# A gated linear attention with a two-layer network on one core: another order of all engines, and v of the later units loaded through ScalarE's queue

## The chip, the cores and the metric

The kernel runs on 1 core of one Trainium2 chip. The metric is the device time of one execution in microseconds, the median over several runs. The core has five engines that run their own instruction lists in order and meet through semaphores: TensorE (PE, with its weight loads PEld), VectorE (DVE), ScalarE (ACT), GpSimd (POOL) and SyncE (SP), which here only issues transfers. Transfers run on 16 DMA engines.

## The reference

```python
# q, k, v, f_logit: [4, 8, 768, 48] float32
f = 1.0 / (1.0 + np.exp(-f_logit))
state = zeros((B, H, D, D)); y = zeros_like(q)
for t in range(S):
    state = f[:, :, t, :, None] * state + np.einsum('bhd,bhe->bhde', k[:, :, t], v[:, :, t])
    y[:, :, t] = np.einsum('bhd,bhde->bhe', q[:, :, t], state)
# x: the heads side by side, [3072, 384]; w_in [384, 2048]; w_out [2048, 384]
x = y.transpose(0, 2, 1, 3).reshape(B * S, H * D)
h = x @ w_in
out = np.maximum(0.01 * h, h) @ w_out
```

The forget gate f is different for every time step, head and channel, so the state is a decayed sum of outer products of k and v.

## The kernel before

The recurrence is computed in chunks of 128 time steps. A chunk needs the cumulative sum of log f (a matmul with a triangular matrix), k and q scaled by the exponentials of it, the scores k q under a causal mask, their product with v, and the product of q with the state before the chunk. The state at a chunk's end is carried to the next chunk of the same batch. Every 256 rows of the attention's result go through the two layers of the network, with a leaky relu between them.

The work is cut into 12 units of 256 rows. Units 0 to 3 are the first two chunks of one batch each (a "paired" unit, in which a partition holds two neighbouring time steps); units 4 to 11 are one chunk of two batches each. In step names the first number is the unit and the second the half (2 is both).

- `Lf`, `Lk`, `Lq`, `Lv` load f_logit, k, q, v of a unit (196,608 bytes a half) into one of six raw buffers; `WI_i`, `WO_i` load the quarters of the weights into the last two of these buffers, and `CI`, `CO` cast them to bf16.
- `ge`, `gl` (ScalarE, L211, L223) make log f; `cs` (PE, L232 to L243) sums it; `dec` (ScalarE, L251 to L257) makes the exponentials; `k`, `q` (VectorE or GpSimd, L263) scale; `v` (GpSimd, L268 to L277) casts v.
- `tk`, `tq`, `ck`, `cq` transpose k and q of units 0 to 3 through PE and copy them out (L296, L309, L311); for units 4 to 11 `xk`, `xq` (SP, L316) transpose by DMA.
- `sc` (PE, L332, L339) makes the scores, `mk` (VectorE, L349, L353) masks them, `mx` and `ms` (PE, L370) multiply by v and by the state, `xt` copies the result out.
- `pt` (PE, L435, L440) makes k v, `sf` (VectorE) and `sb` (GpSimd) update the state.
- `up` (PE, L468: 6 matmuls of 256 columns) is an eighth of the first layer of a unit, `pr` (ScalarE, L473) its relu, `dn` (PE, L480: 4 matmuls of 384 columns) a quarter of the second layer for 128 rows, `ob` copies the result out, `st` (SP, L515) stores it. `dh`, `oh`, `sh` do the last 128 rows in two column halves.
- `F_n` (PE, L133) are n matmuls on a constant whose result nobody reads. `zk`, `zv`, `zs`, `c0`, `pm`, `ut` set constants, among them the pair mask (`pm`).

Nothing plans at run time: the text `order` lists all steps, and each step is written out when its word is read. So the order of words is the order on each engine and in SP's queue. A number after `@` is the PSUM bank; a last number 0, 1 or 2 of `ck`, `cq`, `xt`, `ob`, `CI`, `CO` picks VectorE, ScalarE or GpSimd, and of `k`, `q`, `pm`, `zv`, `zs` 0 is VectorE and 1 GpSimd. Between engines the framework sets semaphores where a step reads or overwrites what another wrote. Each transfer also waits for the landing of the one that stands eight places before it, since eight semaphores are shared in turn.

```python
for word in order.split():
    word, _, at = word.partition("@")
    name, *numbers = word.split("_")
    parts[name](*[int(n) for n in numbers], *[int(n) for n in at.split(".") if n])
```

Of the kernel before, what the change touches and what calls it, by code (L numbers as in the profile page):

```python
# [15 lines left out]
def kernel(  # L16
# [134 lines left out]
    def raw(j, x):  # L151
        return (raw_fk if x in "fk" else raw_qv)[j % NB][:, "fkqv".index(x) % 2]

    def by_pair(t):
        return t.rearrange("t a h d -> t (a h d)").rearrange("t (h s d) -> t h s d", s=2, d=D)

    def load(x):
        def go(j, a):
            if paired(j):
                h = slice(0, H) if a == 2 else slice(4 * a, 4 * a + 4)  # L160
                nc.sync.dma_start(out=by_pair(raw(j, x))[:, h].rearrange("t h s d -> t h (s d)"),  # L161
                                  in_=srcs[x][j, h, 0:2 * C, :].rearrange("h (t s) d -> t h (s d)", s=2))
            else:
                c, h = units[j]
                nc.sync.dma_start(out=raw(j, x)[:, a],
                                  in_=srcs[x][2 * h + a, :, c * C:(c + 1) * C, :].rearrange("h t d -> t h d"))
        return go
# [393 lines left out]
    xt_4_1_1 up_5_5@3 Lf_8_1 Lf_9_0 sb_5_0 q_6_2_0 sf_4_1 Lq_8_1 xt_4_0_0 pr_5_5 pr_5_4 Lv_7_1 Lk_7_0 sb_4_1 up_5_6@4
    cs_7_1@7 k_6_2_0 Lk_7_1 sf_4_0 ob_2_0_0 dec_7_1 up_5_7@3 up_5_2@0 pr_5_6 sb_4_0 k_7_2_1 q_7_2_0 up_5_0@6 up_5_1@7
    pr_5_3 up_4_2@4 pr_5_0 up_4_6@2 up_4_1@1 up_4_4@5 pt_5_1@6 pr_5_1 up_4_0@7 xk_6 sf_5_1 pr_4_1 Lv_7_0 Lv_6_1 xq_6
    pr_5_7 up_4_7@1 pr_4_2 xk_7 v_7_2 pr_5_2 sb_5_1 xq_7 pr_4_0 ge_8_2 up_4_3@3 up_4_5@4 Lf_10_1 dn_5_0_0@6 pr_4_4
    dn_5_0_1 Lf_10_0 st_2_0 st_3_0 gl_8_2 pr_4_3 cs_8_0@0 pr_4_5 pr_4_7 pt_7_0@7 dn_4_0_0@5 dn_4_0_1 sf_7_0 pr_4_6
    dn_5_0_2 ge_9_2 dn_5_0_3 sc_6_1@3.4 dec_8_0 sc_6_0@1.7 sc_7_0@2.0 dn_4_0_2 mk_6_0_0 dn_4_0_3 Lf_11_1 mk_6_0_1
    mk_6_1_0 mk_7_0_0 ob_4_0_1 mk_6_1_1 ob_5_0_1 ge_10_2 dn_4_1_0@1 pt_7_1@7 cs_8_1@3 Lf_11_0 st_2_1 Lq_8_0 Lk_8_0
    gl_9_2 dn_4_1_1 v_6_2 dn_4_1_2 sc_7_1@5.2 gl_10_2 mx_6_0@6 Lq_9_0 mk_7_0_1 Lq_9_1 mk_7_1_0 mk_7_1_1 mx_6_1@4
    mx_7_0@0 xt_6_1_1 mx_7_1@5 xt_6_0_1 Lk_9_1 xt_7_0_0 cs_9_1@2 dn_4_1_3 sf_7_1 dn_5_1_0@4 ge_11_2 Lk_8_1 Lk_9_0
    st_3_1 Lv_9_1 up_6_5@6 pt_6_0@0 dec_8_1 ob_4_1_0 pr_6_5 xt_7_1_1 up_6_1@7 up_6_4@1 gl_11_2 sf_6_0 up_7_0@3  # L570
    cs_9_0@6 Lv_9_0 up_7_2@0 up_7_1@5 dec_9_1 Lv_10_1 up_7_5@2 q_8_2_0 dec_9_0 pr_7_0 pr_7_1 pt_6_1@6 up_7_4@3
    up_6_0@5 pr_6_4 up_7_3@1 pr_6_0 sb_7_0 Lk_11_1 q_9_2_1 sb_6_0 pr_7_2 sf_6_1 xq_8 Lv_10_0 Lv_8_1 k_8_2_0 up_6_2@6
    up_6_7@5 pr_7_4 up_7_6@0 pr_7_3 cs_10_1@3 dn_5_1_1 pr_6_1 dn_5_1_2 cs_11_0@1 pr_6_7 pr_7_6 dn_7_1_0@7 up_6_3@5
    up_7_7@0 dn_5_1_3 sb_7_1 k_9_2_1 xk_8 st_4_1 dec_11_0 pr_6_2 pr_7_5 dec_10_1 Lv_8_0 v_8_2 ob_5_1_0 dn_7_1_1
    Lq_11_1 Lk_11_0 sc_8_1@1.6 Lq_10_0 xk_9 sc_8_0@2.3 mk_8_1_0 dn_7_1_2 pt_8_1@4 sb_6_1 mk_8_0_0 xq_9 dn_6_0_0@1
    Lk_10_1 Lq_10_1 st_4_0 pr_7_7 pr_6_3 dn_6_0_1 pt_8_0@0 dn_6_1_0@5 mk_8_0_1 st_5_1 up_6_6@2 dn_6_1_1 Lk_10_0
    pr_6_6 sf_8_1 mk_8_1_1 v_9_2 sf_8_0 dn_6_1_2 dn_6_0_2 cs_10_0@3 Lq_11_0 Lv_11_1 sc_9_0@4.6 sc_9_1@0.2 dn_7_1_3
    mk_9_0_1 mk_9_1_0 cs_11_1@6 st_5_0 Lv_11_0 dn_6_1_3 mk_9_0_0 ob_7_1_0 dec_10_0 pt_9_0@3 mk_9_1_1 dn_6_0_3 sb_8_0
    mx_8_1@0 dec_11_1 q_11_2_1 k_10_2_1 mx_9_1@4 mx_9_0@6 xt_9_1_1 sf_9_0 ob_6_0_0 xq_11 mx_8_0@7 xt_8_0_0 q_10_2_0
    xt_9_0_1 dn_7_0_0@2 st_6_0 pt_9_1@3 xt_8_1_0 up_9_0@4 sf_9_1 dn_7_0_1 up_9_1@1 up_8_4@6 pr_9_0 xq_10 up_9_5@7  # L580
# [47 lines left out]
```

## Time and profile before

| | |
|---|---|
| median of 3 runs | 183.21 us (181.9, 183.21, 185.36) |
| profiled execution, its own time | 180.78 us |
| its span, first to last instruction | 179.0 us |
| busy: PE, ACT, DVE, POOL | 167.6, 108.1, 82.5, 72.3 us |
| granted TensorE clock | 1.000 over the span |
| read from HBM, written | 25.17 MB, 4.72 MB |
| instructions | 5543 |

The profile is one execution, taken by the hardware's profiler; all durations are read from it. Its own time is 1.78 us longer than its span, which is what lies before the first and after the last instruction. The runs beside it were timed without the profiler. A row of a timeline gives the start and length in us, engine, line, operation, what it writes and reads, and how many alike follow each other; in brackets stands how long the engine was idle before it and what ended that. "SPq" is SP's queue, where a row is the time that the issue of a transfer took, not the transfer. In the rows by line, three numbers with strokes are the shortest, median and longest duration in ns.

### The profile page before, as it was taken

What the parts mean: (1) busy time and instruction counts of PE and PEld (TensorE: products, weight loads), DVE (VectorE), ACT (ScalarE), POOL (GpSimd) and SP (SyncE); (2) the same over time, 40 slices, a digit from 0 to 9 for tenths busy, and PEclk for the clock granted to TensorE, in tenths of its full rate; (3) what the DMA queues carried; (4) which work ended last, traced back from release to release, by engine and by line L of the source; (5) the groups of instructions that cost most, each with busy time, mean ns of one, the idle gap of its engine ahead of it and who ended that gap; (6) DMA issues with size and microseconds to landing.
All of it is one profiled execution on the core that took longest, in us unless ns stands there. A gap on an engine that the chain in (4) does not pass through costs nothing.

```text
span 179.0 us, 5543 instructions
## 1 busy us (share of the span) xinstructions
PE 167.6 (94%) x2302; PEld 131.0 (73%) x2302; DVE 82.5 (46%) x172; ACT 108.1 (60%) x234; POOL 72.3 (40%) x143
## 2 busy tenths in 40 slices
PE   5698989999999999999799999977999999999993
PEld 1456779997567875899656898654798897786772
DVE  7299997644615305684047731363933910110001
ACT  3979766887266992586946878703338354451330
POOL 5177884566303950544570048082499100000000
PEclk9999999999999999999999999999999999999999
DMA  5999999998998999989899989999979000110204
GB/s 149 302 319 346 299 355 291 270 405 275 189 221 188 205 231 190 236 167 218 153 190 267 201 193 211 231 155 249 210 169 245 2 4 0 48 44 0 88 4 176
DMA packets 105961, 34.44 MB, mean 192 GB/s; under 512 B 100688, under 2 KB 103888, under 8 KB 105936
## 3 DMA queue, kind: packets, MB, share of 16 engines
q1 hardware_dynamic: 105936, 34.09, 79.4%
q8 instruction: 18, 0.29, 0.7%
q14 instruction: 7, 0.06, 0.1%
HBM read 25.17 MB, written 4.72 MB: 167 GB/s over the span
## 4 chain that ended last, share of the span: by engine, by line
PE 70%; DMA 12%; SPq 8%; issue 3%; DVE 3%; POOL 2%; ACT 0%; POOLq 0%; DVEq 0%
PE ps L468 31%; PE ps L480 27%; DMA raw_qv<-in_v_dram 7%; SPq L161 5%; PE ps L370 5%; DMA qT<-qh 5%; PE ps L339 2%; SPq L316 2%; POOL vb L268 1%; PE ps L240 1%; PE ps L440 1%; PE ps L296 1%; DVE wm L349 1%; PE ps L435 1%; DVE qh L263 1%
## 5 line engine op out<-in xcount | busy, mean ns | idle before, releaser
L473 ACT ACTIVATE gT<-ps 128x512 bf16<-128x512 f32 x96 | 52.7, 614 | 31.1 <-PE ps L468 28.9
L468 PE MATMUL ps<-xT,w_in 128*128 128x256 bf16 x576 | 69.7, 273 | 0.1
L480 PE MATMUL ps<-w_out,gT 128*128 128x384 bf16 x368 | 67.0, 326 | 0.0
L468 PEld LDWEIGHTS <-w_in 128*128 128x128 bf16 x576 | 61.7, 114 | 3.1 <-POOL w_in L184 0.2
L480 PEld LDWEIGHTS <-gT 128*128 128x128 bf16 x368 | 34.8, 98 | 19.4
L353 DVE TENSOR_TENSOR wm<-ps,ut 128x512 bf16<-128x512 f32 x32 | 20.1, 684 | 15.8 <-PE ps L339 15.6
L491 DVE COPY osb<-ps 128x384 f32<-128x384 f32 x13 | 7.2, 557 | 29.6 <-PE ps L480 28.7
L460 POOL CAST sb<-sf 64x192 bf16<-64x192 f32 x40 | 17.0, 425 | 4.5 <-DVE sf L450 2.4
L263 POOL TENSOR_TENSOR qh<-raw_qv,at 128x384 bf16<-128x384 f32 (+1 forms) x7 | 9.6, 1364 | 22.7 <-DMA raw_fk<-in_k_dram 11.8
L268 POOL CAST vb<-raw_qv 128x384 bf16<-128x384 f32 (+1 forms) x16 | 10.6, 663 | 16.1 <-DMA raw_qv<-in_v_dram 16.0
L452 DVE TENSOR_TENSOR sf<-sf,ps 64x192 f32<-64x192 f32 x32 | 11.2, 349 | 12.3 <-PE ps L440 10.6
L251 ACT ACTIVATE em<-ps 128x384 bf16<-128x384 f32 x24 | 12.0, 500 | 7.5 <-PE ps L240 3.9
L457 POOL TENSOR_TENSOR sf<-sf,end 128x192 f32<-128x192 f32 x16 | 8.8, 550 | 15.8 <-DVE sf L452 13.7
L422 ACT CAST xT<-ps 128x384 bf16<-128x384 f32 x16 | 7.9, 517 | 10.1 <-PE ps L370 9.0
L211 ACT ACTIVATE e<-raw_fk 128x384 f32<-128x384 f32 (+1 forms) x16 | 10.8, 692 | 3.1 <-DMA raw_fk<-in_f_logit_dram 3.1
L252 ACT ACTIVATE at<-ps 128x384 bf16<-128x384 f32 x24 | 12.1, 504 | 0.0
L263 POOL TENSOR_TENSOR kh<-raw_fk,em 128x768 bf16<-128x768 f32 (+1 forms) x7 | 10.7, 1541 | 3.2 <-DMA raw_fk<-in_k_dram 2.3
L263 DVE TENSOR_TENSOR qh<-raw_qv,at 128x768 bf16<-128x768 f32 (+1 forms) x9 | 8.4, 935 | 5.9 <-ACT at L252 4.1
L489 ACT COPY osb<-ps 128x384 f32<-128x384 f32 x10 | 4.9, 491 | 10.1 <-PE ps L480 6.1
L223 ACT ACTIVATE lf<-e 128x384 bf16<-128x384 f32 (+1 forms) x16 | 10.9, 693 | 0.1
L349 DVE TENSOR_TENSOR wm<-ps,pair_mask 128x512 bf16<-128x512 f32 x16 | 10.2, 684 | 1.2 <-PE ps L332 1.0
L263 DVE TENSOR_TENSOR kh<-raw_fk,em 128x384 bf16<-128x384 f32 (+1 forms) x9 | 7.2, 801 | 4.4 <-ACT at L252 2.8
(82 smaller groups left out, 163.3 us busy)
## 6 DMA issues: line engine op xcount, KB each, us to landing
out_dram<-osb SPq DMA_DIRECT2D x23, 192.0 KB, 2.5
raw_fk<-in_f_logit_dram SPq DMA_DIRECT2D x18, 192.0 KB, 4.0
raw_qv<-in_q_dram SPq DMA_DIRECT2D x18, 192.0 KB, 3.7
raw_fk<-in_k_dram SPq DMA_DIRECT2D x18, 192.0 KB, 3.9
raw_qv<-in_v_dram SPq DMA_DIRECT2D x18, 192.0 KB, 3.8
raw_qv<-in_moe_w_in_dram SPq DMA_DIRECT2D x2, 768.0 KB, 6.9
raw_fk<-in_moe_w_in_dram SPq DMA_DIRECT2D x2, 768.0 KB, 9.0
raw_fk<-in_moe_w_out_dram SPq DMA_DIRECT2D x2, 768.0 KB, 7.2
```

The lines of the kernel that those rows point to most:

```text
L223: nc.scalar.activation(dst, src, AF.Ln, bias=1.0)
L251: nc.scalar.activation(ems[j % 2][:, a], t[:, 0:H * D], AF.Exp, scale=1.0)
L252: nc.scalar.activation(ats[j % 2][:, a], t[:, 0:H * D], AF.Exp, scale=-1.0)
L263: eng.tensor_mul(heads(j, to[j % NR], a)[:, :, :, 0:D], raw_heads(j, x, a), decays(j, by, a))
L268: nc.gpsimd.tensor_copy(out=heads(j, vb, a), in_=raw_heads(j, "v", a))
L349: nc.vector.tensor_mul(w.rearrange("t (s p) n -> t s p n", s=2), src.rearrange("t (s p n) -> t s p n", s=2, p=2), pair_mask[:, :, None, :] ...
L353: nc.vector.tensor_mul(w, src.rearrange("t (p n) -> t p n", p=P2), ut[:, None, :].to_broadcast([128, P2, 128]))
L452: nc.vector.tensor_add(sf[rows], sf[rows], new)
L460: nc.gpsimd.tensor_copy(out=sb[rows, :, y * D:y * D + D], in_=sf[rows])
L468: nc.tensor.matmul(pm[:, i, :], w_in_of(ff, kk), xTs[j % 3][:, kk].rearrange("t a s -> t (a s)"), start=(kk == 0), stop=(kk == NK - 1))
L473: nc.scalar.activation(gTs[j % 3][:, 2 * g:2 * g + 2, :], pm, AF.Prelu, alpha=0.01)
L480: nc.tensor.matmul(po, gTs[j % 3][:, ff, 128 * a:128 * a + 128], w_out_b[quarter][:, ff % 4, :], start=(ff == 0), stop=(ff == NF - 1))
```

## The change

The function `load` takes a third number: where it is 1, the transfer is issued by ScalarE's queue. Twelve words have it: both halves of v of units 6 to 11. V of units 0 to 5 and all other transfers stay on SP. The text `order` is another one: the same steps on the same units, in another sequence, with some on another engine and bank. Counted over the whole text: SP issues 121 transfers in place of 133; fillers are 21 in place of 14; ScalarE makes 9 of the copies `ck` and `cq` in place of 3, 11 of the `ob` copies in place of 10, and 5 of the casts `CI` and `CO` in place of 7; VectorE makes 7 `ck` and `cq` in place of 13 and 11 casts in place of 6; GpSimd makes the pair mask, and 8 casts in place of 11. GpSimd scales k 9 times in place of 7 and q 5 times in place of 7. The number of stores, transposes, matmuls of the layers and relus is the same.

```diff
     def load(x):
-        def go(j, a):
+        def go(j, a, e=0):
+            queue = nc.scalar if e else nc.sync
             if paired(j):
...
-                nc.sync.dma_start(out=by_pair(raw(j, x))[:, h].rearrange("t h s d -> t h (s d)"),
+                queue.dma_start(out=by_pair(raw(j, x))[:, h].rearrange("t h s d -> t h (s d)"),
...
-                nc.sync.dma_start(out=raw(j, x)[:, a],
+                queue.dma_start(out=raw(j, x)[:, a],
...
     order = """
-    zk_0 Lf_1_2 Lf_0_1 ge_1_1 Lq_0_1 zv_1_0 gl_1_1 ge_1_0 ge_0_1 c0 zk_1 zs_1_0 zs_2_0 zk_2 zv_0_1 pm_0 gl_1_0 Lk_1_2
-    F_7@1 cs_1_1@0 dec_1_1 gl_0_1 k_1_1_0 cs_1_0@1 Lq_1_2 Lk_0_1 Lf_0_0 Lv_1_2 Lf_2_2 Lk_0_0 Lq_0_0 F_1@3 cs_0_1@2
...
+    Lf_0_1 zs_2_1 zk_0 zv_2_0 ge_0_1 Lf_0_0 c0 ge_0_0 gl_0_1 zk_1 zv_0_0 F_7@1 cs_0_1@0 gl_0_0 Lf_1_2 Lk_0_1 ge_1_1
+    Lv_0_1 zv_1_0 Lq_0_1 dec_0_1 pm_1 gl_1_1 cs_0_0@1 k_0_1_0 ge_1_0 dec_0_0 v_0_1 Lv_0_0 q_0_1_0 v_0_0 F_5@3
+    tq_0_1@2 zs_0_1 Lk_0_0 Lf_2_2 cs_1_1@3 gl_1_0 zs_1_0 k_0_0_0 tk_0_1@4 Lq_0_0 ck_0_1_0 dec_1_1 q_0_0_1 cs_1_0@5
...
+    xt_6_1_1 cs_7_1@2 pt_5_0@7 xt_6_0_0 up_6_0@0 ge_8_2 gl_8_2 Lf_9_1 xt_5_1_0 dec_7_0 pr_6_0 dec_7_1 ob_4_0_1 Lq_8_0
+    Lk_8_0 Lq_7_0 pt_5_1@5 up_6_5@4 up_6_2@3 pr_6_2 up_5_7@1 sf_5_0 sf_5_1 cs_8_0@7 pr_6_5 up_5_0@5 Lf_11_0 q_7_2_0
+    up_5_1@0 cs_8_1@2 up_6_4@6 k_7_2_1 sb_5_1 dec_8_1 dec_8_0 up_5_4@3 sb_5_0 st_3_1 pr_5_0 up_5_3@4 up_5_6@2
+    up_5_2@7 up_6_3@5 pr_5_4 pr_5_1 pr_5_6 Lf_10_1 st_4_1 xq_7 Lv_7_1_1 v_7_2 pr_5_3 up_6_1@3 pr_6_1 sb_6_1 pr_6_4
+    ge_9_2 pr_6_3 up_6_6@0 sb_6_0 q_8_2_0 k_8_2_0 gl_9_2 pr_5_7 dn_6_0_0@2 up_5_5@4 dn_6_1_0@3 xk_7 pr_5_2 up_6_7@6
+    dn_6_1_1 dn_5_0_0@5 pr_5_5 dn_6_1_2 xq_8 dn_6_0_1 cs_9_0@1 xk_8 dn_5_0_1 dn_6_0_2 ge_10_2 pr_6_6 pr_6_7 dec_9_0
+    cs_9_1@7 Lv_8_0_1 Lv_8_1_1 sc_7_0@4.0 sc_7_1@6.1 v_8_2 Lf_11_1 dn_6_0_3 dn_5_0_2 dn_6_1_3 ob_6_1_1 mk_7_1_0 mk_7_1_1
+    dn_5_1_0@6 mk_7_0_1 mk_7_0_0 sc_8_1@1.0 sc_8_0@4.3 st_3_0 st_4_0 Lv_9_1_1 Lk_10_0 Lq_9_1 Lk_9_1 dn_5_1_1 mk_8_1_0
...
```

More of the change, by code (lines that the diff above doesn't have):

```diff
@@ L561 @@
[L561 to L580, printed above, removed]
@@ new lines @@
+    cq_0_1_0 ge_2_0 pt_0_2@6.7 dec_1_0 ge_2_1 sc_0_1@0.1 Lq_1_2 sf_0_0 gl_2_1 zk_2 sb_0_0 q_1_0_1 q_1_1_0 tk_0_0@4
+    F_2@3 tq_0_0@2 Lk_1_2 F_2@5 cs_2_1@3 tq_1_1@6 zs_3_1 k_1_0_1 Lv_1_2 ck_0_0_1 cq_0_0_1 mk_0_1_0 sc_0_0@5.4 k_1_1_0
+    cq_1_1_1 gl_2_0 tq_1_0@0 v_1_1 cq_1_0_1 tk_1_1@2 ck_1_1_1 ut mk_0_0_0 mk_0_0_1 F_3@4 tk_1_0@6 sc_1_1@5.0 dec_2_1
+    mk_0_1_1 v_1_0 mx_0_2@4.2 WI_1 CI_1_2_2 ck_1_0_1 mk_1_1_0 mk_1_1_1 xt_0_0_1 sc_1_0@1.3 ms_0 xt_0_1_1 CI_1_0_1
+    Lf_3_2 pt_1_2@6.5 cs_2_0@0 dec_2_0 ge_3_1 ge_3_0 mk_1_0_1 CI_1_1_0 Lk_2_2 Lq_2_2 up_0_2@4 up_0_3@3 mk_1_0_0
@@ new lines @@
+    sf_1_0 WI_0 sb_1_0 Lv_2_2 k_2_0_1 k_2_1_1 CI_0_1_2 mx_1_2@2.1 gl_3_0 gl_3_1 ms_1 sf_0_1 xt_1_0_0 xt_1_1_1 sf_1_1
+    v_2_0 v_2_1 F_2@7 cs_3_0@0 q_2_0_0 cs_3_1@6 q_2_1_0 dec_3_0 pr_0_3 pr_0_2 WI_2 CI_2_1_2 up_1_2@7 tk_2_0@2
+    tk_2_1@5 tq_2_0@1 tq_2_1@0 ck_2_1_0 ck_2_0_0 cq_2_0_1 cq_2_1_0 up_1_3@3 WI_3 sc_2_0@5.4 sc_2_1@2.1 CI_0_2_0
+    CI_0_0_1 mk_2_0_1 up_0_1@0 Lq_3_2 up_1_0@4 mk_2_1_0 mk_2_0_0 mk_2_1_1 pr_1_2 WO_0 CI_2_0_0 up_1_1@7 dec_3_1
+    pr_1_3 up_0_0@2 pt_2_2@6.5 pr_1_1 sf_2_0 CI_3_0_0 CI_3_1_0 CI_2_2_1 pr_1_0 sb_2_0 pr_0_1 mx_2_2@3.1 CI_3_2_2
@@ new lines @@
+    Lf_5_1 Lv_3_2 Lf_5_0 Lf_6_1 Lf_6_0 cq_3_0_0 Lq_4_1 Lv_4_0 Lq_4_0 Lk_4_1 CO_3_2_2 ge_4_2 dn_1_0_2 dn_0_0_2
+    dn_0_1_1 Lk_4_0 Lk_5_0 Lq_6_0 sb_1_1 pr_2_0 v_3_1 v_3_0 CO_3_0_0 CO_3_1_0 k_3_0_0 dn_1_1_3 tk_3_0@5 dn_1_0_3
+    Lq_5_1 cq_3_1_1 ck_3_0_0 ob_1_0_0 sb_0_1 sb_2_1 dn_0_1_2 sc_3_0@2.1 sc_3_1@6.5 ob_1_1_0 pt_3_2@4.0 mk_3_0_1
+    dn_0_0_3 gl_4_2 mk_3_1_0 ge_5_2 sf_3_0 mk_3_1_1 ge_6_2 cs_4_1@1 gl_5_2 cs_4_0@6 dn_0_1_3 dec_4_1 dec_4_0
+    dn_2_0_0@4 ob_0_1_0 mk_3_0_0 cs_5_1@5 dn_2_1_0@1 sb_3_0 k_4_2_1 st_1_0 mx_3_2@3.2 gl_6_2 ms_3 xt_3_1_1 dn_2_1_1
@@ new lines @@
+    up_4_4@6 sf_4_0 pr_4_1 pr_4_4 pt_4_1@5 st_0_0 xq_5 k_6_2_1 dn_3_1_1 Lf_7_0 up_4_6@3 xk_6 xq_6 sf_4_1 ob_2_0_1
+    k_5_2_1 up_4_3@7 dn_3_1_2 dn_3_1_3 pr_4_0 pr_4_3 dn_3_0_3 Lv_5_0 dn_4_0_0@6 sc_6_1@5.4 sc_6_0@2.7 ob_3_0_0 Lv_6_1_1
+    up_4_5@1 mk_6_1_0 Lf_8_1 st_2_1 sb_4_1 xk_5 ge_7_2 gl_7_2 pr_4_6 Lv_5_1 dn_4_1_0@3 mk_6_0_0 Lk_7_1 Lk_8_1 Lq_7_1
+    v_6_2 sb_4_0 pr_4_5 mk_6_0_1 mk_6_1_1 ob_3_1_0 Lf_8_0 Lf_10_0 sb_3_1 dn_4_0_1 dn_4_1_1 pt_6_1@5 st_2_0 Lv_7_0_1
+    up_4_7@2 dn_4_0_2 sc_5_0@1.7 pr_4_7 v_5_2 sc_5_1@4.0 Lk_7_0 Lq_8_1 mk_5_0_0 dn_4_1_2 dn_4_0_3 pt_6_0@2 dn_4_1_3
@@ new lines @@
+    gl_10_2 xt_7_1_0 xt_7_0_0 ob_6_0_1 up_7_3@2 xt_8_1_1 Lq_9_0 Lk_9_0 pr_7_3 pt_7_0@0 up_7_7@3 cs_10_1@1 xt_8_0_1
+    up_7_0@2 dec_9_1 up_8_0@4 up_7_1@7 Lk_10_1 Lq_10_1 sf_7_0 up_7_4@0 Lk_11_1 dec_10_1 Lq_10_0 Lv_9_0_1 Lq_11_1 pr_7_0
+    pr_8_0 sb_7_0 pt_8_0@1 cs_10_0@2 ob_5_1_0 pr_7_7 up_8_6@6 sf_8_0 q_9_2_0 up_7_2@4 up_7_5@3 ge_11_2 k_9_2_1 sb_8_0
+    pr_8_6 pr_7_2 gl_11_2 st_6_0 up_8_3@1 xq_9 up_8_7@6 pr_7_5 pr_7_1 dec_10_0 pr_7_4 up_8_4@4 up_8_1@3 up_7_6@7
+    pt_8_1@2 up_8_2@0 pr_8_1 ob_5_0_0 k_10_2_0 q_10_2_0 xk_9 dn_8_0_0@5 Lk_11_0 pr_8_7 pr_8_4 dn_7_1_0@3 pr_7_6
@@ L593 @@
+    up_11_4@3 dn_9_0_1 dn_10_0_0@5 pr_10_4 up_11_1@6 dn_9_1_1 pr_11_1 dn_10_1_1 up_11_7@2 dn_9_0_2 up_11_3@6 pr_11_0
+    pr_11_7 pr_11_4 pr_11_3 dn_10_0_1 dn_10_1_2 dn_9_1_2 dn_9_0_3 dn_11_0_0@1 dn_10_1_3 dn_9_1_3 dn_10_0_2
+    dh_11_1_0@2 dn_11_0_1 ob_10_1_0 ob_9_1_0 ob_9_0_0 dn_11_0_2 dn_10_0_3 dn_11_0_3 st_9_1 st_8_0 st_9_0 ob_10_0_1
+    ob_11_0_1 dh_11_1_1@3 oh_11_1_0_0 sh_11_1_0 st_10_1 oh_11_1_1_1 st_10_0 st_11_0 sh_11_1_1
     """
```

62 lines of the change are left out of this document (22 added, 40 removed).

## The prediction

> **What bounds the kernel now.** First the page's engine line and queue line, then the windows by stage.
>
> ```profile
> span 179.0 us, 5543 instructions
> PE 167.6 (94%) x2302; PEld 131.0 (73%) x2302; DVE 82.5 (46%) x172; ACT 108.1 (60%) x234; POOL 72.3 (40%) x143
> ...
> q1 hardware_dynamic: 105936, 34.09, 79.4%
> ```
>
> ```profile
> 0.00:25.00 25.00, 19.78 (x394) 13.58 (x395) 20.10 (x55) 19.51 (x50) 16.16 (x47) 1.00 1.00 289
> 25.00:80.00 55.00, 55.00 (x799) 43.57 (x798) 28.74 (x56) 37.37 (x81) 25.30 (x48) 1.00 1.00 245
> 80.00:95.00 15.00, 13.79 (x132) 11.00 (x131) 5.56 (x12) 9.95 (x20) 8.60 (x16) 1.00 0.98 197
> 95.00:110.00 15.00, 15.00 (x246) 13.19 (x244) 7.84 (x15) 12.83 (x29) 4.60 (x7) 1.00 1.00 212
> 110.00:125.00 15.00, 13.13 (x117) 8.66 (x116) 5.63 (x11) 6.16 (x15) 6.31 (x11) 1.00 1.13 209
> 125.00:171.00 46.00, 46.00 (x580) 37.15 (x579) 13.66 (x25) 21.23 (x42) 11.34 (x16) 1.00 0.32 80
> 171.00:179.00 8.00, 4.91 (x46) 3.84 (x44) 0.92 (x2) 1.06 (x3) 0.00 (x0) 1.00 0.28 100
> ```
>
> The columns are the stretch, its length, the busy time of PE, its weight loads, DVE, ACT and POOL, the granted clock, the DMA share and GB/s. PE is the bound: 11.4 of 179.0 us idle, namely 5.2 before 25 us, 1.2 in 80 to 95, 1.9 in 110 to 125, 3.1 in the tail. The DMA share is about 1.00 up to 125 us, so PE and transfers run side by side, both nearly full. No order can save more than the 11.4 us. Which waits are they? PE's timeline, and POOL's beside it:
>
> ```profile
> 89.25 0.33 PE L440 MATMUL ps<-vb,kh 128*128 128x96 bf16 x4 [0.91 <-POOL vb L268]
> 93.04 0.40 PE L339 MATMUL ps<-qT,kT 48*128 48x128 bf16 x8 [0.30 <-DMA qT<-qh]
> 117.26 0.33 PE L440 MATMUL ps<-vb,kh 128*128 128x96 bf16 x4 [0.96 <-POOL vb L268]
> 123.39 0.62 PE L339 MATMUL ps<-qT,kT 48*128 48x128 bf16 x16 [0.91 <-DMA qT<-qh]
> ```
>
> ```profile
> 88.38 0.82 POOL L268 CAST vb<-raw_qv 128x768 bf16<-128x768 f32 x1 [1.81 <-DMA raw_qv<-in_v_dram]
> 116.38 0.82 POOL L268 CAST vb<-raw_qv 128x768 bf16<-128x768 f32 x1 [4.66 <-DMA raw_qv<-in_v_dram]
> ```
>
> The middle loss, 3.1 us, is supply alone: v of units 7 and 8 and the transposed q of units 7 and 9 come late. ScalarE and VectorE cost PE nothing after 25 us.
>
> **Working unit.** PE's own pace comes from the chain of waits and the timeline:
>
> ```profile
> 36.77 1.97 PE ps L468 x18
> 43.82 5.88 PE ps L480 x36
> 97.56 1.74 PE ps L370 x112
> 9.18 0.81 PE L133 MATMUL ps<-filler 128*128 128x512 bf16 x3
> ```
>
> One step of `up` (6 matmuls) is 0.66 us, of `dn` (4) 0.65, a `mx` (28) 0.44, a filler (0.81 - 0.38)/2 = 0.21. Adding every PE step so, the order before holds 162.5 us and the new one 164.0: the same work and 7 more fillers. The difference between a moment of the trace and the PE work ahead of it I call the lag. At 93.0 us it is 93.0 - 82.2 = 10.8; at 123.4 us, 13.2; at the last matmul (174.4 + 1.5 = 175.9) 13.4. So time = PE work + last lag + 3.1 of tail: 162.5 + 13.4 + 3.1 = 179.0.
>
> ```profile
> 40.39 4.41 SPq L165 DMA_DIRECT2D raw_fk<-in_f_logit_dram  x4
> 135.57 30.98 SPq L515 DMA_DIRECT2D out_dram<-osb  x7
> ```
>
> From the first load of unit 4 at 40.39 us to the last transpose the queue issues 91 transfers in 95 us: 1.05 us each. The first of the seven stores closes this stretch.
>
> **The change part by part.** *The order.* Both orders keep every load, transpose and store (133 transfers). What changes is which transfers stand ahead of which PE work. I count for each unit the transfers from unit 4's first load to its last transpose (n), put it at 40.4 + 1.05 n, add 3.3 for that transpose's issue and landing, and subtract the PE work ahead of its first `sc`:
>
> ```
> unit            4     5     6     7     8     9    10    11
> before  n      21    25    44    46    69    76    89    90
>   lag needed  7.3   8.3   8.3   9.8  12.4  13.3  12.7  14.0
> after   n      18    37    32    59    61    82    89    92
>   lag needed  5.1   7.3   6.8   8.4   7.3   6.7   9.1   8.1
> ```
>
> For before, 9.8 and 13.3 at units 7 and 9 stand beside the measured 10.8 and 13.2: the count is good to 1 us. The new order has 97.2 us of PE work ahead of the scores of unit 7 in place of 82.2, 123.1 in place of 110.2 for unit 9 and 132.2 in place of 124.2 for unit 11, with only 13, 6 and 2 more transfers. So the supply asks for a lag of 9.1 at most instead of the 13.4 there is: -4.3 us. Unit 4's first load has 27 transfers ahead of it in place of 30; I leave it at 40.4 and credit nothing for that. The v loads follow the same count (8.3 at most in the new order, unit 11). *The fillers*: +1.5 us, counted as work; in before they lie in early waits, and if these seven lie in waits too they cost nothing (ends 0 and 1.5; I take 1.5, since they stand between steps that are ready soon).
>
> *The start.* Unit 0 goes first and WI_1 is the first weight.
>
> ```profile
> 19.56 1.68 PE L468 MATMUL ps<-xT,w_in 128*128 128x256 bf16 x12
> ...
> 23.40 0.40 PE L296 MATMUL ps<-ident,qh 128*128 128x128 bf16 x4 [0.51 <-DVE qh L263]
> ```
>
> The first `up` starts at 19.6, with 11.7 us of PE work ahead (lag 7.9), and the lag is 8.9 at 23.4. In the new order the first `up` has 11.8 us ahead and waits for v of unit 1 on POOL, then its state product and the sums of unit 2 (0.9 us).
>
> ```profile
> 14.01 0.92 POOL L263 TENSOR_TENSOR qh<-raw_qv,at 128x384 bf16<-128x384 f32 x1
> 14.86 0.74 POOL L460 CAST sb<-sf 64x192 bf16<-64x192 f32 x2
> 16.47 0.50 POOL L268 CAST vb<-raw_qv 128x384 bf16<-128x384 f32 x1 [0.87 <-DMA raw_qv<-in_v_dram]
> ...
> 17.28 0.50 POOL L268 CAST vb<-raw_qv 128x384 bf16<-128x384 f32 x1
> ...
> 18.08 0.77 POOL L126 MEMSET sb<- 128x384 bf16 x2
> ```
>
> From the landing of q of unit 0 (its second half, tenth issue, some 11 us) POOL does three scalings (2.8), a state cast (0.7), a clear (0.8), two v casts (0.8 each, start to start 16.47 to 17.28) and a mask (0.5): until 17.4, or 19 if its scalings take half as long again. The first `up` is then at 18.3 to 20, lag 6.5 to 8.2. That is under 9.1, so it is not the last wait and I put it at 0. If it were 2 us worse it would become the bound.
>
> *Steps that change engine.* ScalarE gets 6 more copies of transposed q and k and one more output copy, and 2 fewer weight casts; VectorE the reverse; the pair mask goes to POOL. All lie before about 55 us, but for the output copy, under ScalarE's idle of 55 - 37.4 = 17.6 us in 25 to 80; without that cover each costs its 0.5 us. Zero.
>
> *Twelve v loads on ScalarE's queue.* The old trace shows no issue on ScalarE. The nearest rows are SP's, the line's and the transposes':
>
> ```profile
> L165 SPq DMA_DIRECT2D raw_qv<-in_v_dram x16: 432/582/1490, 56.3 to 126.6; - x16
> L165 SPq DMA_DIRECT2D raw_fk<-in_f_logit_dram x16: 379/724/2586, 21.3 to 94.1; - x16
> ...
> L316 SPq DMA_TRANSPOSE qT<-qh x8: 1236/1358/3018, 62.0 to 131.5; - x8
> ```
>
> So I let an issue hold ScalarE for 0.38 to 3.0 us, with nothing else on it meanwhile. Near 0.58 is what one v load takes; I take 1.0, for SP is inside an issue of its own most of this time. What stands behind it are relu steps, and PE waits for these by their banks.
>
> ```profile
> 107.52 3.54 ACT L473 ACTIVATE gT<-ps 128x512 bf16<-128x512 f32 x7 [1.01 <-PE ps L468]
> ...
> 146.58 2.56 ACT L473 ACTIVATE gT<-ps 128x512 bf16<-128x512 f32 x5 [0.98 <-PE ps L468]
> ```
>
> Two more relus take 0.98 us, so one is 0.49 and an `up` 0.66: ScalarE gains only 0.17 per step. Laying its steps of the new order beside PE's, three places are tight. Lv_7_1 stands among five relus ahead of dn_6_0_0: it may last 0.74 before PE waits. Lv_9_0 stands ahead of pr_7_0, whose bank cs_10_0 wants: 0.84. Lv_6_1 must land and be cast within 0.3 us of pt_6_1. At 1.0 us: 0.3 + 0.2 + 0.4 = +0.9 us. The pairs Lv_8_0, Lv_8_1 and Lv_9_1, Lv_10_1 stand where ScalarE waits for output tiles, with about 2 us for each. At 0.58 us the term is 0; at 3.0 it is about 8 (2.3 + 2.2 + 2.4 and about 1 in the pairs).
>
> On SP 12 issues of 0.58 us go. That is 7 us of its queue, and I credit nothing: the DMA share of 1.00 says that engines, not issues, were full. [...]
>
> *Sum*: -4.3 (supply) + 1.5 (fillers) + 0.9 (issues) = -1.9 us: a span of 177.1. The profiled execution took 180.78 us for its span of 179.0, and the median of the runs, 183.21, is 1.013 times that. (177.1 + 1.78) x 1.013 = **181.3 us**, 1.0% under before.
>
> **Rivals.** *A, the lag falls to that of the start.* If the transfers get through faster with two queues, the start sets the last lag, about 7.2: 164.0 + 7.2 + 3.1 = 174.3, or 178.5 us by the median (-2.6%). For it: the need of units 5 to 9 is 6.7 to 8.4. Against: unit 10 and 11 need 9.1 and 8.1, and the count overstates by at most 1.
>
> *B, SP waits for ScalarE's loads.* In the new program a transfer waits for the landing of the one eight places before it, and v loads in this ring are issued only when ScalarE's relus let it. SP's later loads and transposes then stand behind them. Lk_9_1, for example, stands eight behind Lv_8_0. If this delays units 9 to 11 by 2 us, the span is 179.1, 183.3 us: no change. For it: the old trace had all in one queue, in order. Against: at these places the table leaves 2 us.
>
> *C, slower: issues on ScalarE last 2.6 us or more.* The place is the three tight spots, the price 8 us at 3.0 (above). Then 177.1 - 0.9 + 8 = 184.2 in the span, 188.4 by the median. It cancels the gain from about 1.8 us per issue and is slower by 2% from about 2.6. For it: SP's own issues reach 2.6 and 3.0 when the DMA engines are full, and they are full up to 125 us. Against: the median of v is 0.58 in that same stretch.
>
> *D, the queue alone matters little and the order brings nothing*: the DMA rate, not the count, sets the lag (13 again): 164 + 13 + 3.1 = 180.1, 184.4 us.
>
> **Chances.** Forecast 0.45, A 0.2, B and D 0.15 together, C 0.2. About 2% is what a measurement of this kernel can tell from no change (its three runs are 181.9 to 185.36). Faster by over 2% (under 179.5): A, and 0.06 of the forecast's width: 0.26. Slower by over 2% (over 186.9): C and a few of B and D: 0.24. Within: 0.50. The range goes from a little under A, where the issues are free, to near C: 177.5 to 187.5. The forecast's own range is 179.5 to 183.5.
>
> **What would show it.** Right: PE idle in 80 to 125 us falls from 3.1 to under 1.5; the first `up` begins between 18.8 and 19.8 us; no wait of PE for vb; ScalarE shows v issues of 0.6 to 1.2 us; the last matmul has 164 us of work and about 9 of lag. Wrong: issues on ScalarE of over 2 us with PE waiting for relus (C); transposes late after SP waited for a landing (B); early PE waits (before 25 us) of over 7 us (the start is the bound).

## The result, and the profile after

The changed kernel takes 184.15 us (median of 18 runs, 182.19 to 187.6) against 182.57 us before (18 runs, 180.57 to 185.79). The ratio is 1.010, with a 95% interval of 1.0069 to 1.0131: slower by 1%, where the forecast was 1.0% faster (181.3 us). The ratio is taken over undisturbed runs of both, so it is not the quotient of the two medians.

The page of the changed kernel, its first lines and its queues (q10 is ScalarE's):

```profile
span 181.2 us, 5551 instructions
...
PE 169.6 (94%) x2309; PEld 132.0 (73%) x2309; DVE 79.5 (44%) x160; ACT 111.0 (61%) x239; POOL 71.3 (39%) x150
...
q1 hardware_dynamic: 93456, 31.73, 74.6%
q10 hardware_dynamic: 12480, 2.36, 7.1%
```

Its windows, with the columns as before:

```profile
0.00:25.00 25.00, 19.85 (x379) 13.29 (x380) 15.98 (x42) 19.36 (x47) 17.02 (x54) 1.00 0.94 262
25.00:80.00 55.00, 54.73 (x737) 43.43 (x736) 23.84 (x49) 38.69 (x83) 25.94 (x44) 1.00 0.98 245
80.00:95.00 15.00, 14.34 (x249) 11.29 (x248) 9.66 (x20) 7.61 (x19) 5.78 (x11) 1.00 1.21 195
...
110.00:125.00 15.00, 13.26 (x220) 10.52 (x218) 8.33 (x17) 7.49 (x17) 4.73 (x7) 1.00 1.06 200
125.00:171.00 46.00, 45.22 (x539) 36.20 (x537) 15.93 (x27) 24.51 (x49) 11.51 (x21) 1.00 0.42 83
```

PE is busy 169.6 of 181.2 us and idle 11.6, as much as before (11.4). The middle loss that the order was to take away is there again: 0.66 us in 80 to 95, 1.74 in 110 to 125, and 0.78 after 125 us, which before had none. PE's timeline says for what it waited:

```profile
20.38 1.50 PE L469 MATMUL ps<-xT,w_in 128*128 128x256 bf16 x12 [0.22 <-ACT w_in L183]
23.25 0.30 PE L371 MATMUL ps<-qT,sb 128*32 128x128 bf16 x8 [0.45 <-issue]
28.77 1.47 PE L469 MATMUL ps<-xT,w_in 128*128 128x256 bf16 x12 [0.27 <-DVE wm L350]
...
84.41 0.33 PE L441 MATMUL ps<-vb,kh 128*128 128x96 bf16 x4 [0.66 <-POOL vb L269]
...
116.66 0.24 PE L371 MATMUL ps<-wm,vb 128*32 128x128 bf16 x4 [1.64 <-POOL vb L269]
...
146.22 0.62 PE L340 MATMUL ps<-qT,kT 48*128 48x128 bf16 x16 [0.78 <-DMA qT<-qh]
...
176.66 1.48 PE L497 MATMUL ps<-w_out,gT 128*128 128x192 bf16 x16
```

With the lag of the prediction: 164.0 of work + 14.1 of lag (178.1 at the last matmul) + 3.1 of tail = 181.2. The lag should have been 9.1. It is 8.6 at the first `up` (20.4 - 11.8). Then come 0.72 us of waits up to 28.8, v of unit 6 (0.66), v of unit 8 (1.64 and 0.10) and q of unit 11 (0.78): 12.5. The other 1.6 is no wait: in the trace the steps take a little longer than the single durations by which I added them.

Two of the three late waits are for v, which is what the change moved. Were the issues on ScalarE long? The rows by line:

```profile
L166 SPq DMA_DIRECT2D raw_fk<-in_k_dram x16: 433/885/2481, 52.6 to 127.9; - x16
L166 ACTq DMA_DIRECT2D raw_qv<-in_v_dram x12: 374/374/595, 66.1 to 141.4; - x12
...
DMA to landing us min/median/max: 2.5/4.3/7.6
```

No: 0.37 us, less than on SP. The chain of waits shows what was long. Followed back from `mx_8_1` at 117.0 us it goes to v of unit 8, and from there to the landing of an output store:

```profile
107.03 2.89 DMA out_dram<-osb
109.92 0.02 issue
109.94 5.69 DMA raw_qv<-in_v_dram
...
115.78 0.82 POOL vb L269
...
117.00 1.13 PE ps L371 x68
```

A load of v needs nothing of a store. What the two share is the completion semaphore, one of eight. In the trace's records both carry the same number (106), and the load's issue waits until the store has landed. ScalarE's timeline at that place:

```profile
107.55 0.18 ACT L258 ACTIVATE end<-ps 128x4 f32<-128x4 f32 x1
108.96 1.41 ACTq L166 DMA_DIRECT2D raw_qv<-in_v_dram  x2
110.90 0.48 ACT L490 COPY osb<-ps 128x384 f32<-128x384 f32 x1 [3.17 <-PE ps L481]
116.22 1.01 ACTq L166 DMA_DIRECT2D raw_qv<-in_v_dram  x2
117.28 0.84 ACT L224 ACTIVATE lf<-e 128x768 bf16<-128x768 f32 x1 [5.89 <-issue]
```

ScalarE was free at 107.73. It stood 1.23 us before Lv_8_0 (until Lf_11_1 had landed, at 108.94), 0.61 before Lv_8_1 (the store, 109.92) and 4.84 before Lv_9_1 (Lq_9_0, landed at 116.20), each time starting 0.02 us after that landing; Lv_7_0 stood 1.32. Together 8.0 us in which ScalarE did nothing. Lv_7_1 too started 0.02 us after the landing of its semaphore's former user (Lf_11_0, 99.62), but there ScalarE had been busy with relus until then. Lf_11_1, the store (st_4_0) and Lq_9_0 even stand behind these loads of v in the text. So in the changed kernel the rule given above, that a transfer waits for the one eight places before it, does not hold by the order of words (in the kernel before it does: its 133 issues carry the eight numbers strictly in turn, and none starts ahead of the landing of the eighth before it): the eight semaphores are handed out in an order in which ScalarE's loads come later than their words, and a load on ScalarE waits for a younger transfer of SP. Half 1 of v of unit 6, behind the wait at 84 us, is late in a simpler way, by its place among ScalarE's steps. The chain of waits there:

```profile
76.56 1.32 PE ps L469 x12
...
77.91 0.01 ACT gT L474
77.92 5.41 DMA raw_qv<-in_v_dram
```

Lv_6_1 stands behind a relu that waits for PE: the v that PE wants goes out only when PE itself has come so far.

My theory (S) after this: the order is good, and ScalarE's queue costs more than it brings, by loads that start late and by ScalarE standing. Rival P: SP's issues set the pace, and the queue change helps. Rival O: the order costs the time, with its start and its fillers.

### The profile page after: what moved, and what is told of

Same layout as the page of the kernel before. It is cut to its first block, busy times and chain, and to the rows that moved or that the text cites. A ratio compares the mean times of both kernels' runs of the same rounds, so it can differ in the third digit from the quotient of the medians.

```text
span 181.2 us, 5551 instructions
## 1 busy us (share of the span) xinstructions
PE 169.6 (94%) x2309; PEld 132.0 (73%) x2309; DVE 79.5 (44%) x160; ACT 111.0 (61%) x239; POOL 71.3 (39%) x150
## 4 chain that ended last, share of the span: by engine, by line
PE 68%; DMA 13%; ACT 8%; SPq 4%; issue 2%; DVE 2%; POOL 1%; ACTq 0%; POOLq 0%; DVEq 0%
PE ps L469 29%; PE ps L481 25%; DMA raw_qv<-in_v_dram 6%; PE ps L371 6%; SPq L162 4%; ACT gT L474 4%; DMA raw_qv<-in_q_dram 3%; DMA qT<-qh 2%; DMA out_dram<-osb 2%; PE ps L340 2%; DVE wm L350 1%; PE ps L497 1%; PE ps L241 1%; PE ps L441 1%; POOL vb L269 1%
## 5 line engine op out<-in xcount | busy, mean ns | idle before, releaser
L474 ACT ACTIVATE gT<-ps 128x512 bf16<-128x512 f32 x96 | 53.4, 625 | 26.0 <-PE ps L469 25.5
L354 DVE TENSOR_TENSOR wm<-ps,ut 128x512 bf16<-128x512 f32 x32 | 20.4, 684 | 19.4 <-PE ps L340 11.4
L269 POOL CAST vb<-raw_qv 128x384 bf16<-128x384 f32 (+1 forms) x16 | 11.2, 701 | 34.3 <-DMA raw_qv<-in_v_dram 22.2
L492 DVE COPY osb<-ps 128x384 f32<-128x384 f32 x12 | 6.5, 553 | 32.0 <-PE ps L481 31.9
L461 POOL CAST sb<-sf 64x192 bf16<-64x192 f32 x40 | 15.1, 377 | 6.3 <-DVE sf L451 4.1
L264 POOL TENSOR_TENSOR kh<-raw_fk,em 128x768 bf16<-128x768 f32 (+1 forms) x9 | 11.8, 1324 | 11.6 <-DMA raw_fk<-in_k_dram 6.1
L458 POOL TENSOR_TENSOR sf<-sf,end 128x192 f32<-128x192 f32 x16 | 9.0, 564 | 17.8 <-ACT osb L490 10.1
L264 DVE TENSOR_TENSOR qh<-raw_qv,at 128x768 bf16<-128x768 f32 (+1 forms) x11 | 9.7, 894 | 7.2 <-DMA raw_qv<-in_q_dram 7.1
L423 ACT CAST xT<-ps 128x384 bf16<-128x384 f32 x16 | 8.4, 535 | 6.8 <-PE ps L371 6.8
L133 PE MATMUL ps<-filler 128*128 128x512 bf16 x21 | 7.5, 493 | 2.8 <-DVE filler L92 2.0
L371 PE MATMUL ps<-wm,vb 64*32 64x128 bf16 (+1 forms) x256 | 8.1, 220 | 1.6 <-POOL vb L269 1.6
```

What stands on the lines that cost most here:

```text
L264: eng.tensor_mul(heads(j, to[j % NR], a)[:, :, :, 0:D], raw_heads(j, x, a), decays(j, by, a))
L269: nc.gpsimd.tensor_copy(out=heads(j, vb, a), in_=raw_heads(j, "v", a))
L354: nc.vector.tensor_mul(w, src.rearrange("t (p n) -> t p n", p=P2), ut[:, None, :].to_broadcast([128, P2, 128]))
L371: nc.tensor.matmul(banks[st[j]["py", i]][32 * r:32 * r + 32, 128 * kk:128 * kk + 128], lhsT, rhs, start=(i, r) not in begun, stop=i in las ...
L461: nc.gpsimd.tensor_copy(out=sb[rows, :, y * D:y * D + D], in_=sf[rows])
L474: nc.scalar.activation(gTs[j % 3][:, 2 * g:2 * g + 2, :], pm, AF.Prelu, alpha=0.01)
```

## The experiments

The ratio to the kernel before is of one chip for each group; between groups it moves by up to 1%, so differences are taken within a group only.

| group | kernel | median us | ratio, 95% interval |
|---|---|---|---|
| 1 | order alone | 180.54 | 0.9874 (0.9824 to 0.9923) |
| 1 | queue alone | 187.66 | 1.0206 (1.012 to 1.0291) |
| 1 | v of unit 8 back on SP | 182.97 | 0.9993 (0.9948 to 1.0038) |
| 1 | fourteen fillers | 185.42 | 1.008 (1.0025 to 1.0136) |
| 2 | stand-ins on ScalarE | 180.66 | 0.9786 (0.9742 to 0.9831) |
| 2 | small loads on ScalarE | 181.96 | 0.9845 (0.9799 to 0.9891) |
| 2 | units 10 and 11 on ScalarE | 181.07 | 0.9693 (0.9615 to 0.9772) |
| 2 | GpSimd's queue | 182.8 | 0.9891 (0.9833 to 0.995) |
| 3 | changed kernel | 186.33 | 1.0078 (1.0023 to 1.0133) |
| 3 | order alone | 180.86 | 0.9789 (0.9732 to 0.9846) |
| 3 | small loads on ScalarE | 182.61 | 0.9903 (0.9864 to 0.9942) |
| 3 | v of unit 8 late, on SP | 188.04 | 1.0204 (1.0148 to 1.0261) |
| 4 | order alone | 180.69 | 0.982 (0.9768 to 0.9872) |
| 4 | order alone, fourteen fillers | 181.58 | 0.9882 (0.9824 to 0.994) |
| 4 | six that did not stand, on ScalarE | 182.3 | 0.988 (0.9805 to 0.9955) |
| 4 | six that stood, on ScalarE | 183.75 | 0.9984 (0.9944 to 1.0023) |

**The order alone, three times.**

```diff
-    ... Lv_6_0_1 ... Lv_8_0_1 Lv_8_1_1 ...
+    ... Lv_6_0 ... Lv_8_0 Lv_8_1 ...
```

> The new order with all loads of v on SyncE's queue. Theory S (the loss after 25 us is late v: on ScalarE the loads of v of units 6 and 8 start after their turn, and PE waits 0.66 us at pt_6_1 and 1.74 us at mx_8_1 for them): both waits go, span 181.2 - 2.4 = 178.8 us, ratio to before about 0.997. Rival P (SP's issues set the pace, so twelve more of 0.6 us push its later loads and transposes back by up to 7 us): PE waits 2 to 4 us more for transposes, ratio 1.02 to 1.03. Rival O (the order itself, by its start and its seven fillers, costs all of it, the queue nothing): ratio stays at 1.010.

> The changed kernel once more, so that it stands beside the next three on one chip. All theories: 1.010 to before, or what this chip makes of it.

> The new order with all v on SyncE's queue, on the same chip as the changed kernel. All theories: 2% to 2.5% under the changed kernel (0.987 against 1.010 before).

> The order alone, again beside the others of this chip: 0.98 to 0.987 to before, by all theories.

Faster than before in all three groups, by 1.3%, 2.1% and 1.8%, and 2.9% under the changed kernel on the same chip (0.9789 against 1.0078). P and O fall, and the 0.997 of S was too careful: it counted on 2.4 us, and the spans are 4.1 us apart (181.2 and 177.1). Of these 4.1, 0.8 arise before 29 us (the first `up` starts at 20.38 and not 20.02 us, and the wait of 0.45 at 23.25 is missing here). The first load on ScalarE's queue goes out at 66.1 us, so this part is not the queue's. Its page and windows in the first group:

```profile
span 177.1 us, 5553 instructions
...
80.00:125.00 45.00, 44.89 (x624) 36.73 (x619) 22.83 (x42) 29.76 (x66) 18.34 (x34) 1.00 1.02 201
125.00:171.00 46.00, 46.00 (x542) 35.92 (x539) 15.78 (x29) 21.27 (x43) 10.02 (x19) 1.00 0.48 103
```

PE is idle 0.11 us from 80 to 171 us, where the changed kernel has 3.2. SP issued both loads of v of unit 8 right behind the transposes:

```profile
105.46 1.28 SPq L317 DMA_TRANSPOSE kT<-kh  x1
106.79 1.26 SPq L166 DMA_DIRECT2D raw_qv<-in_v_dram  x2
```

They landed at 110.1 and 112.4 instead of 112.8 and 115.6. In the other two profiles of this kernel (spans 177.6 and 178.8) PE still waits up to 0.8 us at a time for transposed q or k or for kh; the supply is just enough.

**The queue alone** (the old order, v of units 6 to 11 on ScalarE's queue).

```diff
-    ... Lv_7_1 Lk_7_0 ...
+    ... Lv_7_1_1 Lk_7_0 ...
```

> The old order with v of units 6 to 11 loaded through ScalarE's queue. Theory S: v of units 7 and 8, already late in before (0.91 and 0.96 us), comes later still behind ScalarE's relus and the waits for a free place among the transfers in flight: 1 to 3 us more of PE waits, ratio 1.005 to 1.015. Rival P: SP is freed of 7 us of issues, the waits for the transposed q of units 7 and 9 (0.30 and 0.91 us) go, ratio 0.99 or less. Rival O: 1.000.

2.1% slower, over the 1.5% that S gave at most, though the interval reaches down to 1.2%. So the queue costs in either order. In its profile (span 186.1 us) PE waits 2.20 us for v of unit 8, as S has it; ScalarE issued one load of v there at 118.97 us, 0.02 us after a load of q of SP had landed. The longest wait, 2.77 us for q of unit 5, is not shown to come from the queue: SP was 2.4 us behind the old kernel at 58.70 us already (56.32 there), and the first load on ScalarE's queue went out at 66.42.

**V of unit 8 back on SP, the rest as changed.**

```diff
-    cs_9_1@7 Lv_8_0_1 Lv_8_1_1 sc_7_0@4.0
+    cs_9_1@7 Lv_8_0 Lv_8_1 sc_7_0@4.0
```

> The changed kernel with only the two loads of v of unit 8 back on SyncE's queue. Theory S: they start at about 105.7 us instead of 108.96 and 109.94, the wait of 1.74 us at mx_8_1 goes, span 179.5 us, ratio 1.000. Rival O: 1.010, since another wait takes its place at the next unit.

The ratio is as S gave it (0.9993), but its profile corrects the reason. The span is 180.9 us, not 179.5. The wait for vb is gone, and in its place PE waits 0.86 and 0.36 us ahead of `up` steps, 0.49 at `dn_6_0_0` and 1.07 at `cs_10_0`, all for ScalarE: that another wait takes its place is what rival O had said. The changed kernel itself is not in this group, so what the step gained is not measured. Its waits are not the same in every execution either: in its second profile (group 3, span 188.1 us), where the first has none, PE waits 1.91 us for the relu at `dn_6_0_0`, behind Lv_7_1, besides 2.48 us for v of unit 8.

**Fourteen fillers in the changed kernel, and in the order alone.**

```diff
-    F_5@3 ... F_2@3 ... F_2@5 ... F_3@4
+    F_3@3 ... F_1@5 ... F_1@4
```

> The changed kernel with fourteen fillers as before in place of twenty-one (F_5 becomes F_3, one F_2 goes, F_2 becomes F_1, F_3 becomes F_1). The forecast counted the seven as 1.5 us of work: ratio 1.002. Theory S: they stand ahead of inputs that are late anyway (0.72, 0.75 and 0.80 us of waits before 17 us), the first up still starts at about 20.4 us, and the ratio stays at 1.010; PE's waits before 25 us grow by about 1.5 us.

> The order alone (all v on SyncE's queue) with fourteen fillers in place of twenty-one. The forecast's filler term: 1.5 us less, 0.8% under the order alone. Rival (the fillers lie in waits for inputs of the start that come when they come): the first up starts less than 0.8 us earlier, and the ratio is within 0.4% of the order alone.

Seven fillers fewer bring nothing that shows: 1.008, where the changed kernel has 1.010 and 1.0078 in other groups, and 0.9882 against 0.982 in one group, with intervals that overlap. The first `up` starts at 19.66 us instead of 20.38 in the one, and at 19.79 instead of 20.13 in the other, 0.3 to 0.7 us for 1.5 us of work. The rest lay in waits. S had put all of it in waits, with the first `up` still at about 20.4 us. In the order alone the ratio went up by 0.6 points, more than the 0.4 that the rival allowed.

**Stand-ins and small loads** (all v on SP; where the changed kernel loads on ScalarE, a copy of 0.41 us by the trace, or a load of 192 bytes).

```diff
-            queue = nc.scalar if e else nc.sync
+            queue = nc.sync
+            if e:
+                nc.scalar.copy(out=stand[:, 0:256], in_=filler[:, 0:256])       # stand-ins
+                nc.scalar.dma_start(out=smalls.pop(), in_=v[0, 0:1, 0, :])      # or small loads
```

> All v on SyncE's queue, and where the changed kernel issues a load of v on ScalarE, ScalarE copies 128x256 bf16 (a stand-in of about 0.4 us, the 0.374 us that an issue held it). Theory S (the price is late v and ScalarE standing for a place among the transfers in flight, not the issue): ratio as with the order alone, 0.987 to 0.992. Rival I (ScalarE is so tight that twelve slots of 0.4 us are the price): ratio near 1.005, with PE waits for gT.

> All v on SyncE's queue, and in the same twelve places ScalarE issues a load of 192 bytes that nobody reads. Theory S1 (ScalarE, and SyncE behind it, stand for a free place among the transfers in flight): most of the loss is there, ratio 1.00 to 1.01, ScalarE shows stands of 1 us and more before its loads. Theory S2 (v itself starts late): v is on SyncE, so the ratio is that of the order alone, 0.987 to 0.992.

> All v on SyncE's queue and twelve loads of 192 bytes on ScalarE's, on the same chip as the changed kernel and the order alone. Theory S1 (standing for a place among the transfers in flight is the price): at least half of the way from the order alone to the changed kernel. Theory S2 (late v is the price): within 0.5% of the order alone.

The issue's slot on ScalarE is not the price: the stand-ins have the lowest ratio but one of their group. Small loads cost 0.6 points more than stand-ins (the intervals overlap, and S1 had given 1.00 to 1.01), and in group 3 1.1 points more than the order alone (0.9903 against 0.9789), of the 2.9 of the whole queue change. Their v is on SP; what comes late is what stands behind the small loads. ScalarE's waits from 96 to 120 us in that kernel:

```profile
ACT lf L228 <- DMA raw_fk<-in_k_dram: 4.5, 1, 4.5
ACT osb L494 <- DMA small<-in_v_dram: 3.1, 1, 3.1
ACT gT L478 <- DMA raw_qv<-in_q_dram: 1.3, 1, 1.3
```

A relu (gT) has no use for q, nor log f for k: these are the small loads ahead of them, standing for the semaphore: seven of the twelve start 0.02 us after the landing of its former user. S1, with the standing, has about two fifths of the loss, less than the half that it gave. The rest is left for S2, late v; this is by elimination, not measured.

**Late v alone** (all v on SP, the two loads of unit 8 and their cast moved behind Lk_9_1).

```diff
-    cs_9_1@7 Lv_8_0 Lv_8_1 sc_7_0@4.0 sc_7_1@6.1 v_8_2 Lf_11_1
+    cs_9_1@7 sc_7_0@4.0 sc_7_1@6.1 Lf_11_1
...
-    Lk_10_0 Lq_9_1 Lk_9_1 dn_5_1_1
+    Lk_10_0 Lq_9_1 Lk_9_1 Lv_8_0 Lv_8_1 v_8_2 dn_5_1_1
```

> The order alone, all v on SyncE's queue, with the two loads of v of unit 8 moved behind the load of k of unit 9 (and their cast with them), so that they start at about 110 us as on ScalarE instead of 106, and nothing else moved. Theory S2 (late v is the price): PE waits about 1.7 us for vb ahead of mx_8_1, 0.9% over the order alone. Theory S1: under 0.4% over the order alone, since nothing stands on ScalarE.

It costs 4.15 points over the order alone, not 0.9, because the shift came out larger than meant: SP, with all v to issue, is at Lk_9_1 only at 114.5 us, not at 108.7, and Lv_8_0 goes at 115.8. So this shows that late v costs, and that the change did free SP: at Lk_9_1 it was 4.9 us ahead of the order alone (108.7 against 113.7 us, group 3), though PE drew no use from it. It does not give the size of late v in the changed kernel. Its profile is below, under the hardware.

**Six and six.** ScalarE keeps those loads that did not stand in the changed kernel, or the others.

```diff
# the six that did not stand: 6_0 7_1 9_0 10_0 11_0 11_1 keep their last 1
# the six that stood:         6_1 7_0 8_0 8_1 9_1 10_1 keep their last 1
```

> On ScalarE's queue only the six loads of v that did not stand there in the changed kernel (6_0, 7_1, 9_0, 10_0, 11_0, 11_1); the others on SyncE's. Theory S (standing, and what comes late by it, is the price): within 0.5% of the order alone. Rival P2 (a second queue as such slows the transfers, or each load on ScalarE costs alike): half of the loss, 1.2% over the order alone.

> On ScalarE's queue only the other six loads of v (6_1, 7_0, 8_0, 8_1, 9_1, 10_1), five of which stood 0.6 to 4.8 us there or started late in the changed kernel. Theory S: most of the loss is back, 1.5% to 3% over the order alone, with PE waits for vb at mx_8_1 or for gT. Rival P2: 1.2% over the order alone.

The six that stood cost 1.6 points over the order alone, as S gave, though by the intervals P2's 1.2 is possible too. PE waits 2.51 us for v of unit 8, and ScalarE stands 2.79 us before Lv_8_0, 0.64 before Lv_8_1 (inside the second row) and 5.39 before Lv_9_1:

```profile
106.95 0.18 ACT L258 ACTIVATE end<-ps 128x4 f32<-128x4 f32 x1
109.92 1.45 ACTq L166 DMA_DIRECT2D raw_qv<-in_v_dram  x2
111.41 0.48 ACT L490 COPY osb<-ps 128x384 f32<-128x384 f32 x1 [4.28 <-PE ps L340]
117.28 1.02 ACTq L166 DMA_DIRECT2D raw_qv<-in_v_dram  x2
```

The other six cost 0.6 points, where S gave at most 0.5 and P2 1.2; the intervals leave that open, the profile less so. Lv_7_1, before which ScalarE had not stood, now makes it stand. The chain of waits:

```profile
97.20 3.65 DMA raw_fk<-in_f_logit_dram
...
100.87 0.38 ACTq L166
...
101.30 0.40 ACT gT L474
...
102.44 0.50 PE ps L481 x2
```

ScalarE stood 2.44 us before it, and PE waited 2.17 us for the relu at `dn_6_0_0`. It is its largest wait. The semaphore (number 101) and its former user, Lf_11_0, are the same as in the changed kernel. There Lf_11_0 had landed at 99.62 us, while ScalarE's relus lasted until then; here ScalarE was free at 98.43 and Lf_11_0 landed at 100.85. So whether a load stands is not a property of the load: it depends on whose semaphore it gets, and on which comes first, ScalarE at the load or the landing. The six that "did not stand" were no safe six.

**Two others on a second queue.**

> Only v of units 10 and 11 (four loads, at 116 to 141 us in the changed kernel, after the full stretch of the transfers but for the first) on ScalarE's queue. Theory S: no late v and hardly a stand, ratio 0.987 to 0.993. Rival P2 (the second queue makes all transfers slower by sharing): a third of the loss, ratio near 0.995.

> The new order with v of units 6 to 11 on GpSimd's queue in place of ScalarE's. Theory S: GpSimd has idle time and is the engine that waits for v anyway, and its loads have places of their own, so nothing of PE's stands behind them: ratio 0.985 to 0.995 if an issue takes GpSimd about 1 us. Rival P2 (any second queue costs): 1.01. If an issue takes GpSimd over 3 us, the casts behind it come late and the ratio is over 1.01.

V of units 10 and 11 alone on ScalarE has the lowest ratio, but it rests on two runs; by the medians (181.07 against 180.66) it is no different from the stand-ins, which speaks against P2. GpSimd's queue (`nc.gpsimd` for `nc.scalar`) is dearer than either, within the range that S gave: its loads carry eight semaphores of their own (numbers 111 to 118) and wait for no transfer of SP, but an issue holds GpSimd 0.92 us, the casts come behind it, and PE waits 2.0 us for vb.

## Why the prediction was wrong, by its steps

- *Supply, -4.3 us.* The mechanism was right and the size too large. The order alone takes away most of the 3.1 us of middle waits (PE is idle 0.1, 1.0 and 1.5 us from 80 to 171 us in three profiles): its last lag is 10.1, 10.6 and 11.8 us there, for 13.4 before. The forecast of 9.1 took the whole 13.4 for a need of the transfers; but 9.1 of it stood there before 27 us, 3.1 were waits, and 1.2 were no wait at all. The prediction itself had named 3.1 us as the middle loss, and credited more than that.
- *Fillers, +1.5.* Wrong end: of the two bounds, 0 is nearer, since taking seven away brought no gain that shows. That the two terms together come near is luck: -4.3 and +1.5 make -2.8 us or 1.5% for the order alone, where 1.3 to 2.1% were measured, but one is too large and the other on the wrong side.
- *The start, 0.* The first `up` came at 20.4 us (19.9 to 20.1 in the order alone), later than the 18.3 to 20 of the forecast, with a lag of 8.6. It became the bound, as rival A had it: in the order alone of the first group the lag is 8.8 at 34 us and 9.1 at 83 us without a wait between. A put that lag at 7.2.
- *Engines, 0.* Nothing speaks against it: in the order alone PE waits 0.8 us (ahead of fillers) and 0.3 us for masks and 0.2 us for a cast of the weights, all up to 28 us. No run moved these steps alone.
- *ScalarE's issues, +0.9.* This is the step that failed. In durations it was too careful (0.37 us, not 1.0), and by its own working the term would then be 0. The queue cost 2.9% on one chip. Between the two spans (181.2 and 177.1) it is 3.3 us, that is 4.1 less the 0.8 that arise before the first load on ScalarE. The term priced the issue and not the wait for a semaphore ahead of the issue, nor the landing behind it: Lv_8_0 and Lv_8_1, "about 2 us for each", stood 1.84 us together, the second took 5.69 us to land, and the wait was 1.74. The three tight spots were tight indeed: 0.66 us at `pt_6_1` in the changed kernel, and in other kernels 2.17 at `dn_6_0_0` with Lv_7_1 standing (2.44 + 0.37 less the 0.74 to spare is 2.07) and 1.07 at `cs_10_0`. But the 1.74 us came at `mx_8_1`, where the prediction had seen room. The 0.78 us for q of unit 11 were not followed to a cause.
- *Rivals.* C had the direction and tight places, but not the cause, since no issue was long, and its price of 8 us was more than twice what the queue cost. B had the cause, the shared semaphores, in the wrong direction: it let SP wait for ScalarE's loads, and ScalarE waited for SP's. D is refuted by the order alone.
- *SP's queue, 0.* Crediting nothing for the twelve issues that left SP was right: SP was 4.9 us earlier at Lk_9_1, and PE waited no less. Nor did SP's issues make ScalarE's long, for which the forecast had taken 1.0 us: of the twelve on ScalarE, nine overlapped an issue of SP of 0.57 to 2.68 us: five of these took 0.374 or 0.375 us, as the three that overlapped none, and four 0.425 to 0.595.

All five signs that the prediction named for being right failed. PE's idle time from 80 to 125 us was 2.4 us and not under 1.5; the first `up` began at 20.4 us and not by 19.8; PE had two late waits for vb where none was to be; the issues lasted 0.37 us and not 0.6 to 1.2; and the last lag was 14.1 us and not about 9.

## What to carry to other kernels

Here a transfer on a busy compute engine's queue cost that engine not the issue (0.37 us) but the wait ahead of it (0.61 to 4.84 us before four of the twelve). Before moving one, ask which earlier transfer holds its semaphore or its place, on whichever queue, and what stands behind it on the engine. Credit an order with the waits that it removes, not with the whole distance between a moment of the trace and the work ahead of it. Here the kernel that beats both is the new order with all loads of v left on SP (0.979 to 0.987 of before).
